# Moving relu(k) of a linear-attention kernel from VectorE to GpSimd, behind a new wait

## Chip, cores, metric

The kernel runs on one core of a Trainium2 chip. The metric is the device time of one execution in microseconds (us), median over runs. Single runs of the kernel before spread by up to 3% (197.43 to 203.25 us in eleven runs). A run over 1.5% above the fastest of its kernel is called slow. The experiments ran in three sessions on three chips, each with the kernel before beside it. Engines are PE (TensorE matmul), PEld (its weight load), DVE (VectorE), ACT (ScalarE), POOL (GpSimd). SBUF is the on-chip memory that these engines share; PSUM is the one that matmuls write.

## The reference

Linear attention with an ELU feature map, 32 heads, 2048 positions, width 128, bf16:

```python
phi_q = jnp.where(q > 0, q + 1, jnp.exp(q)) + 1e-6
phi_k = jnp.where(k > 0, k + 1, jnp.exp(k)) + 1e-6
kv  = einsum("bhsd,bhse->bhde", phi_k, v)
z   = einsum("bhsd->bhd", phi_k)
out = einsum("bhqd,bhde->bhqe", phi_q, kv) / (einsum("bhqd,bhd->bhq", phi_q, z)[..., None] + 1e-6)
```

The kernel writes phi as min(exp(x), 1) + 1e-6 plus relu(x), and lets matmuls add the two parts. A column of ones beside v gives z.

## The kernel before

Every operation has a name; `add(engine, name, function, names it waits for)` puts it at the end of that engine's in-order list. For head h: `ek` is exp(k) on ScalarE, `em` min(exp k) on VectorE, `rk` relu(k), `v1` the copy of v beside the ones, `kv` the 32 kv matmuls, `kvs` the copy of their result out of PSUM, `eq`, `rqa`/`rqb`, `emq` the same maps for q, `T` the transposes of q, `nA`/`nC` the numerator matmuls, `rA`/`fA`/`rC`/`fC` reciprocal and eviction of the result.

```python
def emrk(h):
    add("DVE", f"em{h}", ...tensor_scalar(em, em, 1.0, EPS, op0=min, op1=add), [f"ek{h}"])
    add("DVE", f"rk{h}", ...tensor_scalar(rk, k, 0.0, None, op0=max), [f"ldk{h}"] + kv{h-2})
def emq(h):
    add("DVE", f"emq{h}", ...tensor_scalar(emq, emq, 1.0, EPS, op0=min, op1=add), [f"eq{h}"])
def v1(h):                                   # waits: ldv{h}, kv{h-2}, nA{h-3}
    add("POOL", f"v1{h}", ...tensor_scalar(v1, v, 1.0, 0.0, op0=mult, op1=add), dep)
# kv{h} waits for em{h}, rk{h}, v1{h}, kvs{h-1} ...; rqb (half of relu(q)) runs on
# VectorE in three heads of four ("split" heads), all of relu(q) on ScalarE in the fourth
for i in range(NH):                          # the order within each engine's list
    eq(i); rqa(i); kvs(i+1); ek(i+2)         # ScalarE          (first heads cut)
    f(i-1,"A"); rqb(i); emq(i); f(i-1,"C"); emrk(i+2)   # VectorE
    T(i+1); nA(i); nC(i); kv(i+2)            # PE
```

Of the kernel before, what the change touches and what calls it, by code (L numbers as in the profile page):

```python
# [5 lines left out]
ALU = mybir.AluOpType  # L6
P = 128
# [8 lines left out]
class Program:  # L16
# [10 lines left out]
    def add(self, eng, key, fn, deps=(), dma=None, inc=True):  # L27

        name = dma if dma is not None else eng
        if dma is not None or inc:  # L30
            self.count[name] = self.count.get(name, 0) + (16 if dma is not None else 1)
        if key is not None:
            assert key not in self.where, key
            assert dma is not None or inc
            self.where[key] = (name, self.count[name], eng, len(self.ops[eng]))
        self.ops[eng].append((fn, tuple(deps), name, (16 if dma is not None else 1) if (dma is not None or inc) else 0))
# [61 lines left out]
def bass_standalone__linear_attn_elu__prompt_kernel(nc: bass.Bass, q: bass.AP, k: bass.AP, v: bass.AP, out: bass.AP):  # L98
    B, H, S, D = q.shape
    assert D == P and S == 16 * P  # L100
    NT = S // P
    NH = B * H
    bf16, fp32 = mybir.dt.bfloat16, mybir.dt.float32
    N = NT * D
    NC = D + 1
    NI = 8
    NO = 6
    LAG = 2
# [4 lines left out]
    with ExitStack() as es:  # L113
        names = [0]

        def alloc(make, shape, dt):
            names[0] += 1
            return es.enter_context(make(f"la_{names[0]}", shape, dt))
# [5 lines left out]
        sb = lambda shape, dt=bf16: alloc(nc.sbuf_tensor, shape, dt)  # L124
        k_sb, q_sb, v_sb = sb([P, NI, N]), sb([P, NI, N]), sb([P, NI, N])
        em_sb, rk_sb = sb([P, 2, N]), sb([P, 2, N])
        v1_sb = sb([P, 2, NT, NC])
        emq_sb, rq_sb = sb([P, 2, N]), sb([P, 2, N])
        kvs_sb = sb([P, 2, NC])
        rden_sb = sb([P, 2, NT], fp32)  # L130
# [3 lines left out]
        o_ps = alloc(nc.psum_tensor, [P, 6 * 512], fp32)  # L134
        KV0 = 5 * 512 + 2 * NC
        kv_ps = o_ps[:, KV0:KV0 + NC]
        CO = 4 * 512

        def slot(t):
            if t < 12:  # L140
                return 512 * (t // 3) + NC * (t % 3)
            return CO + 512 * ((t - 12) // 2) + NC * ((t - 12) % 2)

        pr = Program(sem)
        add = pr.add
# [9 lines left out]
        add("DVE", "eps2", lambda g: g.memset(epsr[32:33, :], ec), ["eps0"])  # L155
        add("DVE", "ones", lambda g: g.memset(ones[:], 1.0))
        for s in range(2):
            add("DVE", f"v1ones{s}", lambda g, s=s: g.memset(v1_sb[:, s, :, D:NC], 1.0))


        def load(name, dst, src, h, freed):
            dep = [f"{f}{h - NI}" for f in freed] if h >= NI else []
            add("SP", f"ld{name}{h}", lambda e: e.dma_start(
                dst[:, h % NI].rearrange("p (j d) -> p j d", d=D), rows(src, h)), dep, dma=f"{name}{h % NI}")

        def loads(h):
            load("k", k_sb, kf, h, ["ek", "rk"])
            load("q", q_sb, qf, h, ["T"])
            load("v", v_sb, vf, h, ["v1"])
# [9 lines left out]

        for h in range(min(NI, NH)):  # L180
            loads(h)
        for h in range(NH + LAG):
            if h + NI < NH:
                loads(h + NI)
            if h >= LAG:
# [32 lines left out]
        def emrk(h):  # L218
            s = h % 2
            add("DVE", f"em{h}", lambda e: e.tensor_scalar(  # L220
                em_sb[:, s], em_sb[:, s], 1.0, EPS, op0=ALU.min, op1=ALU.add), [f"ek{h}"])
            add("DVE", f"rk{h}", lambda e: e.tensor_scalar(  # L222
                rk_sb[:, s], k_sb[:, h % NI], 0.0, None, op0=ALU.max), [f"ldk{h}"] + ([f"kv{h - 2}"] if h >= 2 else []))

        def emq(h):
            s = h % 2
# [3 lines left out]
        def v1(h):  # L230
            dep = [f"ldv{h}"]
            if h >= 2:
                dep += [f"kv{h - 2}"]
            if h >= 3:
                dep += [f"nA{h - 3}"]
            add("POOL", f"v1{h}", lambda e: e.tensor_scalar(  # L236
                v1_sb[:, h % 2, :, 0:D], v_sb[:, h % NI].rearrange("p (j d) -> p j d", d=D), 1.0, 0.0,
                op0=ALU.mult, op1=ALU.add), dep)

        def T(h):  # L240
            def f(e):
# [5 lines left out]
        def kv(h):  # L247
            def f(e):
                for j in range(NT):
                    for part, src in ((0, em_sb), (1, rk_sb)):  # L250
                        ins = e.matmul(kv_ps, lhsT=src[:, h % 2, j * D:(j + 1) * D], rhs=v1_sb[:, h % 2, j, :],  # L251
                                       start=(j + part == 0), stop=(j == NT - 1 and part == 1))
                return ins
            add("PE", f"kv{h}", f, [f"em{h}", f"rk{h}", f"v1{h}", "v1ones0", "v1ones1"] + ([f"kvs{h - 1}"] if h else [])
                + ([f"fC{h - 3}"] if h >= 3 else []))
# [58 lines left out]
        for h in range(NH):  # L314
            v1(h)
        ek(0)
        T(0)
        warm(30, 512 + 3 * NC)
        emrk(0)
        kv(0)  # L320
        for i in range(NH):
            eq(i)
            if i == 0 and NH > 1:
                rqa(0)
                kvs(0)
                ek(1)
                emrk(1)
                kv(1)
            else:
                rqa(i)  # L330
            if i + 1 < NH:
                kvs(i + 1)
            if i + 2 < NH:
                ek(i + 2)
            if i >= 1:
                f(i - 1, "A")
            rqb(i)
            emq(i)
            if i >= 1:
                f(i - 1, "C")  # L340
            if i + 2 < NH:
                emrk(i + 2)
            if i + 1 < NH:
                T(i + 1)
            nA(i)
            nC(i)
            if i + 2 < NH:
                kv(i + 2)
# [58 lines left out]
```

## Time and profile before

| | before |
|---|---|
| time, median of 2 | 199.69 us (199.21 to 200.17) |
| period, steady part | 5.53 us per head (22.1 us per four heads) |
| busy PE / VectorE / ScalarE / GpSimd | 86 / 82 / 81 / 35% |

The busy times and four groups of the page of before (busy us, mean ns of one, idle time before and its releaser):

```profile
PE 170.6 (86%) x2842; PEld 160.5 (81%) x2842; DVE 161.6 (82%) x254; ACT 160.0 (81%) x129; POOL 68.4 (35%) x38
...
L236 POOL TENSOR_SCALAR la<-la 128x2048 bf16<-128x2048 bf16 x32 | 67.7, 2116 | 109.1 <-PE la L265 97.5
...
L251 PE MATMUL la<-la 128*128 128x129 bf16 x1024 | 65.3, 222 | 5.7 <-DVE la L222 5.4
...
L220 DVE TENSOR_SCALAR la<-la 128x2048 bf16<-128x2048 bf16 x32 | 22.2, 694 | 27.4 <-ACT la L190 27.4
...
L222 DVE TENSOR_SCALAR la<-la 128x2048 bf16<-128x2048 bf16 x32 | 22.0, 687 | 0.0
```

L236 is the v copy, L251 kv, L220 min(exp k), L222 relu(k). No engine is full. What repeats is a ring of dependences, seen in the timeline of before (start us, duration us; L190 is exp(k), L215 the kv copy, L227 the min of exp(q)):

```profile
84.89 1.90 ACT L190 ACTIVATE la<-la 128x2048 bf16<-128x2048 bf16 x1
85.04 0.68 DVE L227 TENSOR_SCALAR la<-la 128x2048 bf16<-128x2048 bf16 x1
...
86.82 0.69 DVE L220 TENSOR_SCALAR la<-la 128x2048 bf16<-128x2048 bf16 x1 [0.28 <-ACT la L190]
...
87.43 0.69 DVE L222 TENSOR_SCALAR la<-la 128x2048 bf16<-128x2048 bf16 x1
...
87.80 2.08 POOL L236 TENSOR_SCALAR la<-la 128x2048 bf16<-128x2048 bf16 x1 [3.45 <-PE la L265]
...
88.18 2.02 PE L251 MATMUL la<-la 128*128 128x129 bf16 x32
...
90.24 0.28 ACT L215 ACTIVATE la<-la 128x129 bf16<-128x129 f32 x1 [0.77 <-PE la L251]
90.41 1.90 ACT L190 ACTIVATE la<-la 128x2048 bf16<-128x2048 bf16 x1
```

Follow it: exp(k) from 84.89, min(exp k) at 86.82, relu(k) at 87.43, kv at 88.18, kv copy at 90.24, the next exp(k) at 90.41. That is 5.52 us from exp(k) to exp(k), the period of 5.53 within rounding. The v copy lies in the shadow. Note its 2.08 us: it begins while relu(k) runs on VectorE. Where nothing runs beside it, at the start of the execution, it takes 1.90.

### The profile page before, as it was taken

How to read it: one execution, taken by the hardware profiler on the slowest of the kernel's cores; microseconds unless marked ns; L12 is line 12 of the kernel's file. 1: busy time of each engine (PE TensorE's matmuls, PEld its weight loads, DVE VectorE, ACT ScalarE, POOL GpSimd, SP SyncE). 2: the span in 40 equal slices, each digit the busy share in tenths (PEclk: the TensorE clock that was granted, in tenths of full speed). 3: DMA queues.
4: the chain of work that ended last, by engine and by line, in shares of the span. 5: the costliest groups of instructions: out<-in, count | busy, mean ns of one | idle time of the engine just before them, and what ended most of it. 6: DMA issues, size and time to landing. Idle time of an engine off the chain costs nothing.

```text
span 197.3 us, 6384 instructions
## 1 busy us (share of the span) xinstructions
PE 170.6 (86%) x2842; PEld 160.5 (81%) x2842; DVE 161.6 (82%) x254; ACT 160.0 (81%) x129; POOL 68.4 (35%) x38
## 2 busy tenths in 40 slices
PE   6948999988898899988898889988898889988850
PEld 6938889888897889888897889888897889988850
DVE  0213899899989999899989999899989999899774
ACT  4563789988898889988898889988898889998530
POOL 1333343322344444332344444432344444431000
PEclk9997999999999999999999999999999999999985
DMA  6999999999999999999999999999999622222133
GB/s 228 346 418 411 412 404 407 410 404 416 416 411 422 412 416 419 411 420 414 414 420 413 419 418 414 419 414 417 416 415 394 246 116 110 106 106 105 61 130 137
DMA packets 18603, 67.52 MB, mean 342 GB/s; under 512 B 2064, under 2 KB 2192, under 8 KB 18576
## 3 DMA queue, kind: packets, MB, share of 16 engines
q1 hardware_dynamic: 18576, 67.12, 84.4%
q8 instruction: 22, 0.36, 0.7%
q14 instruction: 5, 0.04, 0.1%
HBM read 50.33 MB, written 16.78 MB: 340 GB/s over the span
## 4 chain that ended last, share of the span: by engine, by line
ACT 37%; PE 33%; DVE 22%; DMA 3%; issue 2%; POOL 1%; SPq 0%
ACT la L190 21%; PE la L251 18%; DVE la L299 9%; ACT la L202 6%; ACT la L194 6%; DVE la L220 6%; PE la L243 5%; PE la L263 5%; PE la L265 5%; DVE la L222 4%; DMA la<-in_v_dram 3%; ACT la L215 3%; DVE la L207 2%; DVE la L293 1%; POOL la L236 1%
## 5 line engine op out<-in xcount | busy, mean ns | idle before, releaser
L236 POOL TENSOR_SCALAR la<-la 128x2048 bf16<-128x2048 bf16 x32 | 67.7, 2116 | 109.1 <-PE la L265 97.5
L299 DVE TENSOR_TENSOR la<-la 128x1536 bf16<-128x1536 f32 x64 | 78.4, 1224 | 2.2
L251 PE MATMUL la<-la 128*128 128x129 bf16 x1024 | 65.3, 222 | 5.7 <-DVE la L222 5.4
L251 PEld LDWEIGHTS la<-la 128*128 128x128 bf16 x1024 | 59.7, 98 | 10.2 <-DVE la L222 7.1
L265 PE MATMUL la<-la 128*128 128x129 bf16 x512 | 66.7, 221 | 0.0
L263 PE MATMUL la<-la 128*128 128x129 bf16 x512 | 66.6, 220 | 0.0
L194 ACT ACTIVATE la<-la 128x2048 bf16<-128x2048 bf16 x32 | 59.8, 1869 | 3.7 <-PE la L243 3.7
L190 ACT ACTIVATE la<-la 128x2048 bf16<-128x2048 bf16 x32 | 60.9, 1902 | 1.9 <-DMA la<-in_k_dram 1.9
L265 PEld LDWEIGHTS la<-la 128*128 128x128 bf16 x512 | 49.8, 97 | 0.0
L263 PEld LDWEIGHTS la<-la 128*128 128x128 bf16 x512 | 47.6, 98 | 0.0
L243 PE MATMUL la<-la 128*128 128x128 bf16 x512 | 35.0, 222 | 12.7 <-DVE la L207 11.5
L220 DVE TENSOR_SCALAR la<-la 128x2048 bf16<-128x2048 bf16 x32 | 22.2, 694 | 27.4 <-ACT la L190 27.4
L243 PEld LDWEIGHTS la<-la 128*128 128x128 bf16 x512 | 29.6, 99 | 18.0 <-DVE la L207 15.5
L202 ACT ACTIVATE la<-la 128x1024 bf16<-128x1024 bf16 (+1 forms) x32 | 39.6, 1238 | 0.0
L259 PE MATMUL la<-la 128*128 128x3 bf16 (+1 forms) x192 | 32.5, 169 | 2.2 <-DVE la L227 2.2
L215 ACT ACTIVATE la<-la 128x129 bf16<-128x129 f32 x32 | 9.0, 280 | 23.0 <-PE la L251 23.0
L222 DVE TENSOR_SCALAR la<-la 128x2048 bf16<-128x2048 bf16 x32 | 22.0, 687 | 0.0
L227 DVE TENSOR_SCALAR la<-la 128x2048 bf16<-128x2048 bf16 x32 | 21.8, 683 | 0.0
L259 PEld LDWEIGHTS la<-la 128*128 128x128 bf16 x192 | 19.0, 99 | 2.4 <-DVE la L227 2.4
L207 DVE TENSOR_SCALAR la<-la 128x1024 bf16<-128x1024 bf16 x24 | 16.3, 681 | 0.0
L293 DVE RECIPROCAL la<-la 128x12 f32<-128x12 f32 x64 | 12.9, 201 | 2.5 <-PE la L265 2.5
L308 PE MATMUL la<-la 128*128 128x120 bf16 x90 | 7.6, 268 | 1.5 <-POOL la L149 1.5
(13 smaller groups left out, 9.9 us busy)
## 6 DMA issues: line engine op xcount, KB each, us to landing
la<-in_k_dram SPq DMA_DIRECT2D x32, 512.0 KB, 15.0
la<-in_q_dram SPq DMA_DIRECT2D x32, 512.0 KB, 15.0
la<-in_v_dram SPq DMA_DIRECT2D x32, 512.0 KB, 15.2
out_dram<-la SPq DMA_DIRECT2D x31, 512.0 KB, 15.1
out_dram<-la SPq DMA_DIRECT2D x1, 384.0 KB, 2.3
out_dram<-la SPq DMA_DIRECT2D x1, 128.0 KB, 2.1
```

The source lines that it names most:

```text
L190: add("ACT", f"ek{h}", lambda e: e.activation(em_sb[:, h % 2], k_sb[:, h % NI], ACT.Exp), [f"ldk{h}"] + ([f"kv{h - 2}"] if h >= 2 else []))
L194: add("ACT", f"eq{h}", lambda e: e.activation(emq_sb[:, h % 2], xT[:, :], ACT.Exp), [f"T{h}"] + ([f"nC{h - 2}"] if h >= 2 else []))
L202: add("ACT", f"rqa{h}", lambda e: e.activation(rq_sb[:, h % 2, 0:n], xT[:, 0:n], ACT.Relu), [f"T{h}"] + ([f"nC{h - 2}"] if h >= 2 else []))
L220: add("DVE", f"em{h}", lambda e: e.tensor_scalar(em_sb[:, s], em_sb[:, s], 1.0, EPS, op0=ALU.min, op1=ALU.add), [f"ek{h}"])
L222: add("DVE", f"rk{h}", lambda e: e.tensor_scalar(rk_sb[:, s], k_sb[:, h % NI], 0.0, None, op0=ALU.max), [f"ldk{h}"] + ([f"kv{h - 2}"] if h ...
L236: add("POOL", f"v1{h}", lambda e: e.tensor_scalar(v1_sb[:, h % 2, :, 0:D], v_sb[:, h % NI].rearrange("p (j d) -> p j d", d=D), 1.0, 0.0, o ...
L243: ins = e.transpose(xT[:, j * P:(j + 1) * P], q_sb[:, h % NI, j * D:(j + 1) * D], ident[:])
L251: ins = e.matmul(kv_ps, lhsT=src[:, h % 2, j * D:(j + 1) * D], rhs=v1_sb[:, h % 2, j, :], start=(j + part == 0), stop=(j == NT - 1 and par ...
L259: e.matmul(_ap(o_ps[:, :], slot(tiles[0]) + D, [[NC, n]]), lhsT=ones[:], rhs=epsr[:, 0:n], start=True, stop=False, skip_group_check=True)
L263: e.matmul(o, lhsT=emq_sb[:, s, t * P:(t + 1) * P], rhs=kvs_sb[:, s, :], start=False, stop=False, skip_group_check=True)
L265: ins = e.matmul(o, lhsT=rq_sb[:, s, t * P:(t + 1) * P], rhs=kvs_sb[:, s, :], start=False, stop=True, skip_group_check=True)
L299: add("DVE", f"f{which}{h}", lambda e: e.tensor_tensor(out=_ap(o_sb[:, :, :, :], ob + t0 * D, [[n * D, nb], [D, n], [1, D]]), in0=_ap(o_ps ...
```

## The change

The intent: take relu(k) off VectorE and out of that ring. To make room on GpSimd, v is copied as half as many 32-bit words. A new wait on the min of exp(q) keeps GpSimd's work from starting under VectorE's own operations.

```diff
-        v1_sb = sb([P, 2, NT, NC])            # NC = 129
+        v1_sb = sb([P, 2, NT, NV])            # NV = 130: rows of whole 32-bit words
 def emrk(h):
-            add("DVE", f"rk{h}", lambda e: e.tensor_scalar(
-                rk_sb[:, s], k_sb[:, h % NI], 0.0, None, op0=ALU.max), ...)
 def v1(h):
+            if h >= 4:
+                dep += [f"emq{h - 2}"]
-            add("POOL", f"v1{h}", lambda e: e.tensor_scalar(..., 1.0, 0.0, op0=ALU.mult, op1=ALU.add), dep)
+            add("POOL", f"v1{h}", lambda e: e.tensor_copy(
+                v1_sb[:, h % 2, :, 0:D].bitcast(i32), v_sb[:, h % NI]....bitcast(i32)), dep)
+            add("POOL", f"rk{h}", lambda e: e.tensor_scalar(
+                rk_sb[:, h % 2], k_sb[:, h % NI], BIG, 0.0, op0=ALU.min, op1=ALU.max), [f"ldk{h}"] + ...)
```

GpSimd works in order, so relu(k), which stands behind the copy, is held by the new wait as well.

More of the change, by code (lines that the diff above doesn't have):

```diff
@@ L105, in bass_standalone__linear_attn_elu__prompt_kernel @@
     NC = D + 1
+    NV = D + 2
+    i32 = mybir.dt.int32
+    BIG = 3.4028234663852886e38
     NI = 8
@@ L157, in bass_standalone__linear_attn_elu__prompt_kernel @@
         for s in range(2):
-            add("DVE", f"v1ones{s}", lambda g, s=s: g.memset(v1_sb[:, s, :, D:NC], 1.0))
+            add("DVE", f"v1ones{s}", lambda g, s=s: g.memset(v1_sb[:, s, :, D:NV], 1.0))
         def load(name, dst, src, h, freed):
@@ L221, in emrk @@
                 em_sb[:, s], em_sb[:, s], 1.0, EPS, op0=ALU.min, op1=ALU.add), [f"ek{h}"])
-            add("DVE", f"rk{h}", lambda e: e.tensor_scalar(
-                rk_sb[:, s], k_sb[:, h % NI], 0.0, None, op0=ALU.max), [f"ldk{h}"] + ([f"kv{h - 2}"] if h >= 2 else []))
         def emq(h):
@@ L235, in v1 @@
                 dep += [f"nA{h - 3}"]
-            add("POOL", f"v1{h}", lambda e: e.tensor_scalar(
-                v1_sb[:, h % 2, :, 0:D], v_sb[:, h % NI].rearrange("p (j d) -> p j d", d=D), 1.0, 0.0,
-                op0=ALU.mult, op1=ALU.add), dep)
+            if h >= 4:
+                dep += [f"emq{h - 2}"]
+            add("POOL", f"v1{h}", lambda e: e.tensor_copy(
+                v1_sb[:, h % 2, :, 0:D].bitcast(i32), v_sb[:, h % NI].rearrange("p (j d) -> p j d", d=D).bitcast(i32)), dep)
+            add("POOL", f"rk{h}", lambda e: e.tensor_scalar(
+                rk_sb[:, h % 2], k_sb[:, h % NI], BIG, 0.0, op0=ALU.min, op1=ALU.max), [f"ldk{h}"] + ([f"kv{h - 2}"] if h >= 2 else []))
         def T(h):
@@ L250, in f @@
                     for part, src in ((0, em_sb), (1, rk_sb)):
-                        ins = e.matmul(kv_ps, lhsT=src[:, h % 2, j * D:(j + 1) * D], rhs=v1_sb[:, h % 2, j, :],
+                        ins = e.matmul(kv_ps, lhsT=src[:, h % 2, j * D:(j + 1) * D], rhs=v1_sb[:, h % 2, j, 0:NC],
                                        start=(j + part == 0), stop=(j == NT - 1 and part == 1))
```

## The prediction

> **What bounds the kernel now.** The timeline repeats every 22.1 us per four heads, 5.53 us per head, from about 24 to 180 us. The groups show no saturated engine: VectorE is 82% busy, ScalarE 81%, PE 86%. It is a ring of dependences, which the timeline gives for a head with the split relu(q): exp(k) 1.80 us on ScalarE, then min(exp k) 0.13 + 0.61 on VectorE, relu(k) 0.60 + 0.15, the kv matmuls 2.05, the kv copy 0.17 on ScalarE, then the next exp(k). Sum 5.5, the measured period. GpSimd's v copy (2.08 us median, 1.90 with nothing else running) is off it.
>
> **What the change does.** It takes relu(k) (0.60 us of issue spacing, 22 us in all) out of VectorE and out of this ring, which alone would leave 4.9 us; PE (about 5.05 us of back-to-back work per head) and ScalarE (4.95) would then bound, near 5.1. On GpSimd the v copy halves its element count. Estimate from 1.90 us for 2048 elements: about 1.0 us for 1024 words. relu(k) has the old v copy's form, two scalar operations over 2048 bf16, so 1.9 us. Together 2.9 us, which fits in 5.5 us. "GPSIMD Engine Reference", section 3.1, of the Trainium skill states one rate for bodies of up to two operations, 1.03 cycles per element; the 1.90 us agree.
>
> **But the gate builds a new ring.** Both now begin only when the min of exp(q) of head i ends (call it E), and kv(i+2) needs both. E + 0.1 + 2.9 + kv 2.1 + kv copy 0.2 + exp(k) 1.9 + min(exp k) 0.65 + reciprocal 0.26 + eviction 1.67 + half relu(q) 0.6 + min(exp q) 0.68 leads to E two heads later: about 11.1 us, 5.55 per head. So even with no contention nothing is gained in the steady part; only the ungated start gains a little.
>
> **And the ports.** "SBUF — State Buffer", section "Who interferes with whom", of the Trainium skill says that VectorE operations in a two-port mode and GpSimd operations exclude each other for the whole instruction. The trace agrees in one direction: GpSimd's v copy takes 2.08 or 2.40 us where it starts under VectorE's relu(k), and the excess is that operation's remaining time; no VectorE victim is shown. min(exp k) wants to start about 1.1 us after E, just as the v copy ends. If it gets in between, relu(k) starts 0.55 later and the ring is 11.7 (5.85 per head). If relu(k) gets in first, min(exp k) is held about 1.9 us, and a one-head ring closes: 0.1 + 2.9 + 0.65 + 0.26 + 1.67 + 0.6 + 0.68 = 6.9 us (6.3 in heads without the half relu(q)). Laying the engines' orders out with these durations, it alternates or stays in the second: 5.9 to 6.6 per head, against 5.53, over some 28 heads.
>
> **Prediction.** 207 us, range 190 to 222. Faster by over 2%: 0.25; within 2%: 0.20; slower by over 2%: 0.55.
>
> **What would show it.** Right: VectorE's busy share falls, except that some min(exp k) last 1 to 2.5 us instead of 0.69; VectorE or PE's kv matmuls wait for GpSimd's relu(k); GpSimd 92 to 100 us busy; ScalarE's kv copy waits longer for PE; the chain of waits runs through GpSimd, min(exp k), eviction, min(exp q). Wrong: min(exp k) stays 0.69 us, the kv matmuls wait for min(exp k) alone, and the period is near 5.1.
>
> **What would make it wrong.** relu(k) or the word copy much faster than estimated (2.0 us together would give about 5.3 per head without contention, some 188 us); VectorE not held by GpSimd (then 193 to 197); or min(exp k) reliably going first. The order of two requests within 0.05 us of each other decides much, hence the width.

## The result

| | before | after |
|---|---|---|
| time, median of 2 | 199.69 us | 225.35 us (225.26 to 225.45) |
| ratio of fast runs, 95% interval | | 1.131 (1.119 to 1.143) |
| period, steady part | 5.53 us | 6.49 us (25.94 us per four heads) |

A ratio compares the fast runs of the two kernels in the same rounds, so it is not quite the ratio of the medians quoted. The change made the kernel 13% slower. The accounting closes: 6.49 - 5.53 = 0.96 us more per head, over 27 steps between the 28 heads that have the new wait, is 26 us; the medians differ by 25.7.

The page of after, the same lines. L239 is the word copy, L241 relu(k) on GpSimd, L223 min(exp k), L255 kv, L228 the min of exp(q):

```profile
PE 168.9 (76%) x2842; PEld 159.4 (71%) x2842; DVE 186.6 (83%) x222; ACT 160.7 (72%) x129; POOL 93.4 (42%) x70
...
L255 PE MATMUL la<-la 128*128 128x129 bf16 x1024 | 65.0, 221 | 34.5 <-DVE la L223 33.4
L223 DVE TENSOR_SCALAR la<-la 128x2048 bf16<-128x2048 bf16 x32 | 66.2, 2070 | 28.5 <-ACT la L193 28.4
...
L239 POOL COPY la<-la 128x1024 int32<-128x1024 int32 x32 | 33.2, 1039 | 114.0 <-DVE la L228 102.3
...
L241 POOL TENSOR_SCALAR la<-la 128x2048 bf16<-128x2048 bf16 x32 | 60.6, 1895 | 0.0
```

VectorE lost 22 us of relu(k) and is busier than before. Nearly the whole excess is one group: min(exp k) went from a mean of 694 to one of 2070 ns, the same instruction on the same data, 44 us more in all. The timeline of after shows where its time goes (L297 and L303 are reciprocal and eviction, L210 the half relu(q)):

```profile
74.82 0.68 DVE L228 TENSOR_SCALAR la<-la 128x2048 bf16<-128x2048 bf16 x1
...
75.57 1.04 POOL L239 COPY la<-la 128x1024 int32<-128x1024 int32 x1 [3.74 <-DVE la L228]
76.57 1.90 POOL L241 TENSOR_SCALAR la<-la 128x2048 bf16<-128x2048 bf16 x1
76.59 2.42 DVE L223 TENSOR_SCALAR la<-la 128x2048 bf16<-128x2048 bf16 x1 [0.27 <-ACT la L193]
78.94 0.22 DVE L297 RECIPROCAL la<-la 128x12 f32<-128x12 f32 x1
79.19 1.76 DVE L303 TENSOR_TENSOR la<-la 128x1536 bf16<-128x1536 f32 x1
80.86 0.68 DVE L210 TENSOR_SCALAR la<-la 128x1024 bf16<-128x1024 bf16 x1
81.46 0.68 DVE L228 TENSOR_SCALAR la<-la 128x2048 bf16<-128x2048 bf16 x1
...
83.21 1.90 POOL L241 TENSOR_SCALAR la<-la 128x2048 bf16<-128x2048 bf16 x1
...
83.23 2.42 DVE L223 TENSOR_SCALAR la<-la 128x2048 bf16<-128x2048 bf16 x1 [0.27 <-ACT la L193]
...
89.25 1.89 POOL L241 TENSOR_SCALAR la<-la 128x2048 bf16<-128x2048 bf16 x1
89.86 1.82 DVE L223 TENSOR_SCALAR la<-la 128x2048 bf16<-128x2048 bf16 x1 [0.87 <-ACT la L193]
```

relu(k) starts at 76.57 and min(exp k) 0.02 us later. relu(k) ends at 78.47, and min(exp k) ends 0.54 us after that, at 79.01. In the last two lines, a head whose wait is on a min of exp(q) without the half relu(q) before it, min(exp k) starts 0.61 us later relative to relu(k), and again it ends 0.54 us after relu(k) (91.14 and 91.68). So it is not slowed in proportion: it is held until relu(k) is done and then runs at its own pace. The eviction, which reads PSUM, is 1.76 us as before (it doesn't meet relu(k) here, but in experiment 5 it does, at the same 1.76 us). This is what "SBUF — State Buffer", section "Who interferes with whom", of the Trainium skill states: a VectorE operation in a two-port mode and a GpSimd operation take the shared port pair for a whole instruction, and "Issue order, not op shape, decides who blocks." The traces show the exclusion; that the cause of it is this port pair is the page's statement. The trace of before showed only the other direction, the v copy of 2.08 us instead of 1.90: it starts 0.32 us before relu(k) ends at 88.12 and is 0.18 us longer, so the excess is the remaining time less 0.14 us (the prediction has it as the whole of that time).

All 28 heads that have the new wait show a min(exp k) of 1.82 us or more; the four heads without it show 0.69.

Now the ring. From the min of exp(q) at 74.82 to the next at 81.46 is 6.64 us: copy, relu(k), held min(exp k), eviction, half relu(q), min of exp(q). In a head without the half relu(q) it is 6.04. Three of the one and one of the other make 25.96, the 25.94 us within rounding.

The chain of waits of after tells it differently:

```profile
83.23 2.43 DVE la L223
85.66 0.05 issue
85.70 2.02 PE la L255 x32
87.73 0.02 issue
87.75 0.28 ACT la L218
88.04 1.80 ACT la L193
```

It walks the old ring (min(exp k), kv, kv copy, exp(k)) and gives GpSimd 1% of the span. The hold is no wait on a semaphore, and the views of waits don't show it; it appears only as a longer duration of the instruction that is held. The clue is a duration that changed without a change in the operation.

### The profile page after: what moved, and what is told of

It reads as the page before. It is cut to its first block, busy times and chain, and to the rows that moved or that the text cites. A ratio compares the mean times of both kernels' runs of the same rounds, so it can differ in the third digit from the quotient of the medians.

```text
span 223.6 us, 6408 instructions
## 1 busy us (share of the span) xinstructions
PE 168.9 (76%) x2842; PEld 159.4 (71%) x2842; DVE 186.6 (83%) x222; ACT 160.7 (72%) x129; POOL 93.4 (42%) x70
## 4 chain that ended last, share of the span: by engine, by line
DVE 33%; PE 32%; ACT 27%; DMA 3%; issue 2%; POOL 1%; SPq 0%
DVE la L223 28%; PE la L255 27%; ACT la L193 23%; ACT la L218 4%; DVE la L303 3%; DMA la<-in_v_dram 3%; PE la L247 2%; PE la L267 2%; PE la L269 1%; POOL la L241 1%; DVE la L210 1%; DVE la L297 0%; POOL la L239 0%; SPq L166 0%; DVE la L228 0%
## 5 line engine op out<-in xcount | busy, mean ns | idle before, releaser
L255 PE MATMUL la<-la 128*128 128x129 bf16 x1024 | 65.0, 221 | 34.5 <-DVE la L223 33.4
L223 DVE TENSOR_SCALAR la<-la 128x2048 bf16<-128x2048 bf16 x32 | 66.2, 2070 | 28.5 <-ACT la L193 28.4
L255 PEld LDWEIGHTS la<-la 128*128 128x128 bf16 x1024 | 59.5, 98 | 39.6 <-DVE la L223 38.4
L239 POOL COPY la<-la 128x1024 int32<-128x1024 int32 x32 | 33.2, 1039 | 114.0 <-DVE la L228 102.3
L303 DVE TENSOR_TENSOR la<-la 128x1536 bf16<-128x1536 f32 x64 | 78.3, 1224 | 2.2
L269 PE MATMUL la<-la 128*128 128x129 bf16 x512 | 65.8, 220 | 0.0
L267 PE MATMUL la<-la 128*128 128x129 bf16 x512 | 65.8, 219 | 0.0
L241 POOL TENSOR_SCALAR la<-la 128x2048 bf16<-128x2048 bf16 x32 | 60.6, 1895 | 0.0
L218 ACT ACTIVATE la<-la 128x129 bf16<-128x129 f32 x32 | 9.0, 281 | 49.0 <-PE la L255 49.0
L228 DVE TENSOR_SCALAR la<-la 128x2048 bf16<-128x2048 bf16 x32 | 22.1, 692 | 0.0
L210 DVE TENSOR_SCALAR la<-la 128x1024 bf16<-128x1024 bf16 x24 | 16.3, 680 | 0.0
L297 DVE RECIPROCAL la<-la 128x12 f32<-128x12 f32 x64 | 12.6, 197 | 2.8 <-PE la L269 2.6
## 6 DMA issues: line engine op xcount, KB each, us to landing
out_dram<-la SPq DMA_DIRECT2D x1, 128.0 KB, 2.1
```

The lines of the kernel that those rows point to most:

```text
L223: add("DVE", f"em{h}", lambda e: e.tensor_scalar(em_sb[:, s], em_sb[:, s], 1.0, EPS, op0=ALU.min, op1=ALU.add), [f"ek{h}"])
L239: add("POOL", f"v1{h}", lambda e: e.tensor_copy(v1_sb[:, h % 2, :, 0:D].bitcast(i32), v_sb[:, h % NI].rearrange("p (j d) -> p j d", d=D).b ...
L241: add("POOL", f"rk{h}", lambda e: e.tensor_scalar(rk_sb[:, h % 2], k_sb[:, h % NI], BIG, 0.0, op0=ALU.min, op1=ALU.max), [f"ldk{h}"] + ([f ...
L255: ins = e.matmul(kv_ps, lhsT=src[:, h % 2, j * D:(j + 1) * D], rhs=v1_sb[:, h % 2, j, 0:NC], start=(j + part == 0), stop=(j == NT - 1 and ...
L267: e.matmul(o, lhsT=emq_sb[:, s, t * P:(t + 1) * P], rhs=kvs_sb[:, s, :], start=False, stop=False, skip_group_check=True)
L269: ins = e.matmul(o, lhsT=rq_sb[:, s, t * P:(t + 1) * P], rhs=kvs_sb[:, s, :], start=False, stop=True, skip_group_check=True)
```

## The experiments

The theory: relu(k) behind the new wait takes the port just ahead of min(exp k), and together they close a one-head ring. Rivals: GpSimd's larger amount of work costs whatever the wait; only the late arrival of relu(k) costs and the port plays no part; the word copy or the wait alone costs. Edits are against the changed kernel. All runs gave correct results.

### 1. No wait

```diff
-            if h >= 4:
-                dep += [f"emq{h - 2}"]
```

> The new wait on the min of exp(q) two heads back is taken away, all else of the change stays. If the wait is what costs (it closes the ring copy, relu(k), min(exp k), eviction, half relu(q), min(exp q) and puts relu(k) just ahead of min(exp k) at the shared port): about 187 us, period near 5.3 us per head, min(exp k) back at 0.69 us, and now the min of exp(q) held by GpSimd's relu(k) for about 0.5 us in a head. If the amount of GpSimd work is what costs, whatever the wait: it stays above 215 us.

Measured: 191.85 us median, ratio to before 0.958 (0.953 to 0.963), faster than both kernels, though 5 us above the 187 expected. Two groups of its page (L228 the min of exp(q)):

```profile
L223 DVE TENSOR_SCALAR la<-la 128x2048 bf16<-128x2048 bf16 x32 | 22.2, 694 | 22.7 <-ACT la L193 22.2
L228 DVE TENSOR_SCALAR la<-la 128x2048 bf16<-128x2048 bf16 x32 | 34.1, 1065 | 0.0
```

min(exp k) is free again. The copy now starts about when min(exp k) ends, and relu(k) overruns into the min of exp(q), which is held 0.25 us in split heads (0.93 us long) and 0.85 in the others. GpSimd does exactly the work of the changed kernel, so the amount of work is not the cause. Deleting one wait takes some 33 us off the changed kernel.

### 2. A nudge of 0.1 us

```diff
+            add("POOL", None, lambda e: e.memset(pad[:, 32 * h:32 * h + 32], 0.0), inc=False)
             add("POOL", f"rk{h}", ...
```

> A small GpSimd memset of 32 columns of an unused tile (about 0.1 us) stands between the word copy and relu(k); nothing needs it. In the changed kernel relu(k) starts 0.02 us before min(exp k) is asked for. If the order of these two requests decides: min(exp k) now goes first in every second head or more, lasts 0.69 us there, and the time FALLS to about 206 us (200 to 216) although work was added. If the order does not matter, or GpSimd keeps the port over consecutive instructions: 0.1 us more per head, 226 to 229 us, and min(exp k) stays at 2.4 us or longer.

Measured: 209.96 us, ratio to before 1.048 (1.043 to 1.053). Adding work to the changed kernel took 15 us off it. The timeline of this run (L240 copy, L242 memset, L243 relu(k), L224 min(exp k)):

```profile
91.89 0.13 POOL L242 MEMSET la<- 128x32 bf16 x1
91.97 2.40 POOL L243 TENSOR_SCALAR la<-la 128x2048 bf16<-128x2048 bf16 x1
...
97.22 1.89 POOL L243 TENSOR_SCALAR la<-la 128x2048 bf16<-128x2048 bf16 x1
...
91.93 0.69 DVE L224 TENSOR_SCALAR la<-la 128x2048 bf16<-128x2048 bf16 x1 [0.27 <-ACT la L194]
...
98.66 0.99 DVE L224 TENSOR_SCALAR la<-la 128x2048 bf16<-128x2048 bf16 x1 [0.89 <-ACT la L194]
```

In one head min(exp k) is now 0.04 us ahead, runs free, and relu(k) is held (2.40 us). In the next, min(exp k) arrives late; in every second of these heads it meets the tail of relu(k) (0.99 us), in the others it does not (0.69). The heads alternate, 5.9 us each on average (the copies at 79.27 and, four heads later, 102.85). So the order of two requests 0.02 to 0.04 us apart is worth 15 us here, and GpSimd does not keep the port from one instruction to the next.

### 3. relu(k) always second

```diff
-  ..., op0=ALU.min, op1=ALU.max), [f"ldk{h}"] + ...)
+  ..., op0=ALU.min, op1=ALU.max), [f"ldk{h}"] + ... + ([f"em{h}"] if h >= 4 else []))
```

> relu(k) of head h waits for min(exp k) of the same head (from head 4 on), so that min(exp k) is never held at the port by relu(k). If holding min(exp k) at the port is the whole loss: at or below the kernel before, 190 to 200 us. If the lateness of relu(k) is a loss of its own: the ring exp(k) 1.8, min(exp k) 0.65, relu(k) 1.9 and its start, kv 2.05, kv copy 0.17 closes within one head, about 6.8 us per head, 228 to 233 us, with min(exp k) at 0.69 us and the kv matmuls waiting for GpSimd's relu(k).

Measured: 242.78 us, ratio 1.210 (1.201 to 1.218), slower still, and above the 228 to 233 expected. The timeline (L255 kv, L218 the kv copy):

```profile
90.19 0.69 DVE L223 TENSOR_SCALAR la<-la 128x2048 bf16<-128x2048 bf16 x1 [0.89 <-ACT la L193]
...
90.96 1.89 POOL L241 TENSOR_SCALAR la<-la 128x2048 bf16<-128x2048 bf16 x1 [2.81 <-DVE la L223]
...
93.00 2.00 PE L255 MATMUL la<-la 128*128 128x129 bf16 x32 [2.10 <-POOL la L241]
...
95.04 0.28 ACT L218 ACTIVATE la<-la 128x129 bf16<-128x129 f32 x1 [1.35 <-PE la L255]
95.21 1.90 ACT L193 ACTIVATE la<-la 128x2048 bf16<-128x2048 bf16 x1
...
97.15 0.69 DVE L223 TENSOR_SCALAR la<-la 128x2048 bf16<-128x2048 bf16 x1 [0.89 <-ACT la L193]
```

In the steady part min(exp k) is not held, yet the ring of the kernel before is back with a 1.9 us relu(k) in it: 0.77 to relu(k), 1.89, 0.15, kv and copy 2.21, exp(k) and start 1.94, in all 6.96 us (97.15 - 90.19). I had summed 6.8. Four heads took longer, 7.4 to 8.2 us; in the stretches 46 to 54, 61 to 69, 146 to 153 and 160 to 168 us that hold them the mean granted clock was 0.78 to 0.81 instead of 1.00 (97 to 104 us), and the kv block at 64.05 took 3.12 us instead of 2.00. They add some 3.3 us to the run. Hence "the hold at the port is the whole loss" is false: a relu(k) that starts this late costs by itself. With the wait this late, letting relu(k) go first and hold min(exp k), 6.49 us per head, is the lesser evil.

### 4. The word copy and the wait, relu(k) back on VectorE

```diff
-            add("POOL", f"rk{h}", ...)
+            add("DVE", f"rk{h}", ...)     # after em{h}, as before
```

> Only the word copy of v and the new wait; relu(k) is back on VectorE. The copy (1.04 us) then ends just about when min(exp k) is asked for. If relu(k) on GpSimd behind the wait is the cause and the copy is not: 198 to 202 us, as before, min(exp k) at 0.69 to 0.8 us. If the wait itself or the word copy costs: above 205 us.

Measured: 199.27 us, ratio 0.993 (0.987 to 1.000), min(exp k) 694 ns. The copy and the wait together cost nothing without relu(k) behind them; each alone was not run.

### 5. The same work, one head earlier

```diff
-            if h >= 3:
-                dep += [f"nA{h - 3}"]
             if h >= 4:
-                dep += [f"emq{h - 2}"]
+                dep += [f"emq{h - 3}"]
   # and relu(k): ... + ([f"em{h - 1}"] if h >= 4 else [])
```

> The same GpSimd work, but each operation waits one head earlier: the word copy of head h for the min of exp(q) three heads back (instead of two), relu(k) of head h for min(exp k) of head h-1; the older wait on the numerator matmuls is dropped. So the copy runs in the stretch after min(exp q), relu(k) in the stretch between min(exp k) and the next min(exp q), in which VectorE only evicts from PSUM. If place and lateness of the wait are the whole cause: 185 to 191 us, min(exp k) and min(exp q) both near 0.69 us, a little below the run with no wait. If GpSimd behind any wait on VectorE costs: above 200 us.

Measured: the two fast runs of four took 191.08 and 190.85 us (the slow ones 194.65 and 196.48), so no interval was formed; run 8 repeats it. The timeline (L237 copy, L239 relu(k)):

```profile
88.98 0.69 DVE L223 TENSOR_SCALAR la<-la 128x2048 bf16<-128x2048 bf16 x1 [0.41 <-ACT la L193]
...
92.32 0.69 DVE L228 TENSOR_SCALAR la<-la 128x2048 bf16<-128x2048 bf16 x1
...
89.76 1.89 POOL L239 TENSOR_SCALAR la<-la 128x2048 bf16<-128x2048 bf16 x1 [0.90 <-DVE la L223]
...
90.05 1.76 DVE L301 TENSOR_TENSOR la<-la 128x1536 bf16<-128x1536 f32 x1
...
93.07 1.04 POOL L237 COPY la<-la 128x1024 int32<-128x1024 int32 x1 [1.42 <-DVE la L228]
```

relu(k) lies between min(exp k) and the min of exp(q), the copy after the latter, and neither min is held. The eviction at 90.05 runs beside relu(k) and is not longer. GpSimd still waits for the end of a min on VectorE, though relu(k) now for another one than the copy, and the edit also drops the older wait on `nA`. The GpSimd work is the same; its place and its head changed.

### 6. The wait on relu(k) alone

```diff
-            if h >= 4:
-                dep += [f"emq{h - 2}"]         # on the copy
   # and relu(k): ... + ([f"emq{h - 2}"] if h >= 4 else [])
```

> Only relu(k) waits for the min of exp(q) two heads back; the word copy starts as in the kernel before. If the period of the changed kernel is the one-head ring min(exp q), copy 1.0, relu(k) 1.9, min(exp k), eviction, half relu(q), min(exp q): the ring loses the copy's 1.0 us, period 5.6 instead of 6.5 us per head, 195 to 202 us, with min(exp k) held about 0.9 us instead of 1.8 (lasting some 1.4 to 1.6 us). If another chain sets the period: less than 10 us gained against the changed kernel's 225 us.

Measured: 199.30 us, ratio 0.999 (0.993 to 1.006). This run tests the ring by its length. The timeline (L239 relu(k), L223 min(exp k); the releaser named for relu(k) is the reciprocal just after the min of exp(q), inferred by the profiler's reader, while the wait in the edit is on that min):

```profile
86.36 1.90 POOL L239 TENSOR_SCALAR la<-la 128x2048 bf16<-128x2048 bf16 x1 [2.32 <-DVE la L295]
...
92.02 1.90 POOL L239 TENSOR_SCALAR la<-la 128x2048 bf16<-128x2048 bf16 x1 [2.32 <-DVE la L295]
...
87.36 1.44 DVE L223 TENSOR_SCALAR la<-la 128x2048 bf16<-128x2048 bf16 x1 [0.27 <-ACT la L193]
```

The copy's 1.0 us left the ring, and the split head fell from 6.64 to 5.66 us (92.02 - 86.36). min(exp k) is held for the rest of relu(k), 0.75 us, as the end of relu(k) at 88.26 requires. The kernel is then just as fast as before: the 0.60 us taken off VectorE is given back at the port, where min(exp k) is held 0.75 us in three heads of four and 0.15 in the fourth.

### 7. relu(q) split in every head

Edit, against kernel 5: `return h % 4 != 3` becomes `return True`.

> The one-head-early waits, and relu(q) split between ScalarE and VectorE in every head instead of three of four, using the VectorE time that relu(k) left. If ScalarE bounds the unsplit heads (5.5 us there against 5.25 in the others, as the run with no wait showed): 1 to 3 us less than the one-head-early kernel, 183 to 188 us. If VectorE's chain bounds all heads: no change or slower.

Measured: 193.31 us, ratio 0.965 (0.956 to 0.974), not below kernel 5. The period fell only from 5.28 to 5.25 us per head, which is 0.7 us in all and under the noise. My guess that ScalarE held back the fourth heads by a useful amount fell.

### 8 and 9. Kernels 5 and 1 again, five rounds

> The one-head-early kernel again, in five rounds on one chip with the kernel with no wait, because half its earlier runs fell in the slow state. Both held 5.25 us per split head, set by the transposes, numerator matmuls, eviction and half relu(q), not by the port, so: within 1% of the kernel with no wait, 189 to 193 us, and 4 to 6% below the kernel before. If the 0.25 to 0.9 us hold of the min of exp(q) in the kernel with no wait counts: 2 us or more below it.

> The kernel with no wait again, in the same rounds: 190 to 193 us, min(exp k) at 0.69 us, the min of exp(q) at 0.9 to 1.6 us.

Measured: ratio to before 0.962 (0.951 to 0.974) for one head early, 0.963 (0.955 to 0.971) for no wait. The record's verdicts are faster for run 8 and unclear for run 9: only two runs of six and three of six were fast, at 190.7 to 193.0 and 191.0 to 192.7 us. The medians over all runs, 194.25 and 193.36 us, include slow runs. For the kernel with no wait, experiment 1 (four fast runs, ratio 0.958) is the firmer measurement. The two cannot be told apart, so the hold of the min of exp(q) in the kernel with no wait costs nothing that shows. Both beat the kernel before by about 4% and the changed one by about 15%.

One profiled execution of run 8 took 327.23 us. It is left out of all comparisons and described in the last section.

## Why the prediction was wrong, and where it was right

- **The old ring, 5.5 us: right.** Experiment 3 puts GpSimd's relu(k) back into it and gets 6.96, and experiments 1 and 5 take it out and gain.
- **Cost of the GpSimd operations: right.** Estimated 1.0 and 1.9 us, measured 1.04 and 1.89. The difference between them, 1024 elements more though in another operation, is 0.86 us. At the 1.2 GHz of "GPSIMD Engine Reference", section 1, of the Trainium skill that is an estimate of 1.0 cycle per element; section 3.1 states 1.03.
- **Exclusion of VectorE by GpSimd: right**, and shown in both directions: 28 held min(exp k) in the changed kernel, and in experiment 2 a relu(k) of 2.40 us behind a min(exp k).
- **The new one-head ring: right in kind.** Put at 6.9 us in split heads and 6.3 in the others; measured 6.64 and 6.04. Experiment 6 shortened it by the copy and the period followed.
- **The step that failed:** "Laying the engines' orders out with these durations, it alternates or stays in the second: 5.9 to 6.6 per head". I treated who comes first at the port as nearly a toss-up. By my own figures the two patterns mean 210 and 230 us (0.37 and 1.07 us more per head over 28 heads); 207 lies below both (I had given 45% to "faster" or "the same"). It stands for some 0.26 us more per head, where 0.96 was measured. The trace shows relu(k) first, and so the second ring, in all 28 heads: 6.49 us per head. Alternation, at 5.9 us, is what experiment 2 gave, at 210 us. So 207 was nearer to the nudged kernel than to this one.
- **It was no toss-up.** Both requests go back to the same event, the end of the previous min(exp k). From 79.01 us, relu(k) is reached through eviction, half relu(q), min of exp(q) and copy at 83.21; min(exp k) is reached through kv, kv copy and exp(k) at 83.23. The difference of two sums of fixed durations comes out the same, 0.01 to 0.02 us, in every split head but the first (0.17), and in the others relu(k) leads by 0.61 or 0.62. What could not be known blind is its sign, at 0.02 us.
- **The range was also too narrow by my own numbers.** The second pattern's 230 us lies above the 222 on record. The measured 225.35 lay within what I had laid out, but not within what I wrote down.
- **What the views would show: partly wrong.** GpSimd's 93.4 us busy (92 to 100), the long min(exp k) (1 to 2.5 us; 2.42) and the longer wait of ScalarE's kv copy for PE (23.0 us before, 49.0 after) came as said. The kv matmuls wait for min(exp k), not for relu(k) as said. VectorE's busy share did not fall, for a held instruction counts as busy. The chain of waits does not run through GpSimd, for the hold at the port is not seen as a wait.
- **"Even with no contention nothing is gained":** the two-head ring of 5.55 us was an estimate and was not isolated by any run, since no run had the GpSimd work without the port. Experiment 3 shows only that lateness can cost by itself.
- **Left open:** what sets the 5.25 us per head of kernels 1, 5 and 7. From the timeline I would name the ring of q's transposes, numerator matmuls, eviction and half relu(q); in run 7 these lines and the reciprocal make up 84% of the chain that ended last, but no run tests it.

## What to carry to other kernels

When work moves to GpSimd, lay its operations out against VectorE's two-port operations by time, and let the wait that starts it lie a full head ahead of its consumer, as in experiment 5, or leave it out where the data allow, as in experiment 1; here a wait on the engine that needs the same port, just before that engine's next two-port operation, made a ring out of a shortcut. If a duration grows while its operation did not change, look for a shared port before looking at waits. When a race is settled by a few hundredths of a microsecond, predict both outcomes separately and let the range cover both whole; the same outcome may repeat in every iteration.

## What the Trainium skill lacked or had wrong

- "SBUF — State Buffer", section "Who interferes with whom", is right about the exclusion, but does not say what the profile makes of a hold: the held VectorE instruction is recorded as started and longer (2.42 us instead of 0.69), it counts as busy, and the chain of waits gives the engine that holds the port 1% of the span.
- The same page does not say what happens between two GpSimd instructions in a row. In experiment 2 a VectorE operation got in between (91.93, with relu(k) listed at 91.97), and in the changed kernel it did not, when it came 0.02 us after the start of the second one. In experiment 6 the waiting min(exp k) went ahead of the word copy listed 0.07 us after the end of relu(k) (min(exp k) ends at 88.80; the copy, from 88.33, takes 1.37 us instead of 1.04).
- "GPSIMD Engine Reference" has the rate per element used above, but no measured copy of 32-bit words: 1.04 us for 128x1024 int32, against 1.90 for the two-operation form on 128x2048 bf16.
- "TensorE: Matmul & The Clock Gate", Part 1, says that the array reaches its full clock after about 3.4 us of sustained work. In one execution of run 8 (327.23 us) it seems never to have: PE was 96% busy and the kv matmuls together took 128.0 us instead of 64.6 (experiment 5, the same kernel), while VectorE's eviction kept its 1.22 us mean. The granted clock is given as 1.0 for it, but the trace holds no clock record of this execution, so that figure measures nothing. The same Part warns that such records can be unreliable and that the clock has been seen stuck low. The cause was not looked for.
